# Four layers of attention in one hand-ordered kernel: a new order of its instructions, and another way through the last four rows of output

## The chip, the core and the metric

The kernel runs on one core of one Trainium2 chip. Its time is device microseconds (us) of one launch, the median of several runs. The engines of the core each have an instruction stream of their own and meet through semaphores: TensorE (PE, matmuls; PEld is its loading of weights), VectorE (DVE), ScalarE (ACT), GpSimd (POOL) and SyncE (SP), which issues the transfers.

## What is computed

Four times, with two sets of weights in turn, a layer norm, an attention with 32 query heads of 16 dimensions and one head of keys and values, and an output product added to the input. One layer, cut to what matters:

```python
q = (x @ wq).reshape(B, S, H, Dh).transpose(0, 2, 1, 3)      # S 2048, H 32, Dh 16
k = x @ wk
v = x @ wv
scores = jnp.einsum("bhqd,bkd->bhqk", q, k) * (Dh ** -0.5)
p = _softmax(scores, axis=-1)
o = jnp.einsum("bhqk,bkd->bhqd", p, v)
return o.transpose(0, 2, 1, 3).reshape(B, S, H * Dh) @ wo
# used as
x = x + _A_ref(_layernorm(x), A_wq, A_wk, A_wv, A_wo)        # then B, then A, then B
```

x is 2048 x 512 in float32.

## The kernel before

**Tiles.** A layer's 2048 queries are four blocks `b` of 512. A block's heads are four groups `m` of eight. One (layer, block, group) is a pair, and there are 64 of them. For a pair the keys go by in halves; one unit is 128 x 1024 scores: eight small matmuls (64 x 32 pieces of the array, 512 columns each) into one of two score tiles `st`, each of two PSUM banks. ScalarE turns a unit into exponentials in a tile `pt` of SBUF (line 765). TensorE then multiplies these with the values and adds into two banks, `acc[0]` for even heads and `acc[1]` for odd ones (function `pv`). The values' tile has ones beside it, so the same product yields the sum by which the softmax divides; in `acc` each 32 rows hold 16 of values and 16 of sums.

**Two engines for the exponential.** There are 4096 units. For most ScalarE does the work. For some VectorE does it instead: TensorE writes their scores into a bank of their own, `by_v`, in two halves; VectorE reads each half (`exp_first`, line 796) and then works six steps on the unit (`chain`, lines 807 to 815).

**Everything else.** The projections for the next block or layer, layer norm, transposes and output products run in between, in program order of a work list (`plan`). They share one bank, `beside`. A product can be cut in row halves of the array (24 steps, laid beside other small matmuls) or be 12 whole passes of 128 x 128 (`whole`, line 521). VectorE's part of the list evacuates `beside`. Each output row block of 128 rows is a product of 12 passes (four groups `m`, three passes each, since both factors are split in a float16 value and a rest), and `out_add` (line 455) adds it to `x` and sends it out (line 460 in the last layer, by SP's queue).

**The order.** All of this is written out by hand in a string `ORDER`, one letter for each step, and every engine executes its part in that order. The letters that matter here:

- S: a unit of scores and its exponential on ScalarE.
- a to e, l to q: products with the values (E and O in `STEPS` are `acc[0]` and `acc[1]`), with row halves of a list product (M, N) beside them. f to k, r and s also write a half of a unit for VectorE (V, W).
- I: VectorE reads such a half. 0 and 1: one of the six steps for a unit.
- X: the next step of VectorE's list. F: a small whole step of TensorE's list. P: one whole pass.
- G: an evacuation of `acc` into `sum` (lines 902 and 904). D: a step of a division. Q: a load of queries. Y: a touch of `beside` by VectorE, by which the order between the two row halves is known.

**Divisions.** When a pair is complete, its sums are inverted and spread over the rows by transfers (`divide`). For the last pair `divide_last` does it without transfers: with `lo` and `hi`, masks of the rows, VectorE parts values (`ev`) and sums (`den`), and for each of four slices of 128 columns inverts, swaps halves of 16 rows by a shuffle, multiplies, casts to float16 and subtracts for the rest (lines 968 to 972). Then the four last row blocks follow, each as 12 P and an X, all through `beside`. The end of the order before is

```python
"...SSaaSSaaSSaaaaGGDDDDDDDDDDDDDDDDDDDDDDDDPPPPPPPPPPPPXPPPPPPPPPPPPXPPPPPPPPPPPPXPPPPPPPPPPPPXX"
```

The functions that the diff touches and what calls them, with the line numbers of the profile:

Of the kernel before, what the change touches and what calls it, by code (L numbers as in the profile page):

```python
# [23 lines left out]
NL = 4  # L24
# [36 lines left out]
    "aIqS0as0SaaISc0qSaq1Sa0qSaa1SQqq0Saa0ScqSaXaXSGlSXFGrSXaISaXa0SaSaX0aSsaXISaX0SaaXXS0ppp0Sa0QaSb0SaaS0aS"
    "cGoGSqj0SccIScsYSbIpS0ap0Sa0aSb0SaaS0aSaa0SQpaXSaXaSaSabGSppGpSkbISbhSIpaY0Sc0qSa0aSc0Saa0ScqSa0aScSQcaX"
    "SaXSaaSbGpSbpSGkppISahSIap0Sa0aS0dSaY0aScq0SaaS0cSccSQqqqSaXaXSaSabGSbpSGkpISbfSIbp0SaY0aS0aSaa0ScqDS0aa"
    "Sq0qSccDSQcqSaXaXSaSaaSFGSXalXGSppDSaDaDSbpSbbSbSdaYScqSaaSaSQaaSaqSaXaXScGqSXcDXSmGmSqaSqjaISasSaISDa0a"
    "XS0lXSa0aSlrXSaIaXSsXSQaaSSIaaXXSrGSGlXSaDbS0bpSbD0pSbbDSlYDq0ScqSIaa0Si0ScIc0SjcSD1aaXSa0SaaXSa0pSb1bSD"
    "bp0SbSbIaYDSc0qSaDaSDc0Scc0ScqSaXaD0SmSsXaISbb0S0kbISb0bSaDSa0aSjcIScDj0SaaDSc0SaaISa0qSi0aISc0SaaY1Ska0"
    "SaaXSa0SaaXSa0SFISaXa0Sb0ShbISb0pSkb1Sa0aSa1Sc0cSQaISa0aScr0SaaIScGqSjGo0SaSa1a0SapSaIaXSaDXSa0gSIbp0Sha"
    "D1Sa0Saa1Sc0Scc1ScqSc0qSaYIaS0bSaa0SkbISa0hSaISbDaSXa0SaXaS0kbISb0hSa1Sa0aSc1qSa0aSc1qSc0SccSIaY0SkbpISb"
    "0SaaXSa0SaaXSa0jScIc0Si0SccISa0qSjaY1Sa0aSb1Sa0aSbIpSp0bSaa0SkbISQa0pSaaXSa0SaaXSfGSGFISaXaSXkpSaaSbIpSX"
    "bX0b0Sb0ShaY1Sc0qSaaXS0cSaXaSXc0SccISaXqS0as0SaaISaXS0aaSaXS0aaSXa0rSaSIaXaSXaSasSaaISXXS0aa0SP0PSa1aS0P"  # L70
    "PSP1PS0PPSr1PPSP0SPSIaXaS0aSbb0SkaISa0aSkaISa0Sh0aISa0kSaa1Sb0Saa1Sb0SaaY1Scq0ScqScIc0SQcSaXa0SjcSIcc0Sa"
    "r0SaISbGb0Sa0pSpppGSpg0SaaISa0Scc1Sa0qSaaY0Sb0SdaXSaXXSaDXaXSDraISaXXaSDaXXSa0aSaX0sSaaISaXD0Saa0Sa0SaXa"
    "XS0FSaXSaDaXSaXrSDFISXaaDSaXSXaaXD0SFSXsaISaXm0SFSaXS0aaSrXaISa0aSD0kbISb0Shb1Sb0SbaY1ScDqSa0aScDq0ScqSI"
    "cqDSaXaXSa0SaaSXQa0SaaXS0aSaXlGSFGsSXmISaX0aSfXDSIaaXX0Sc0qSc0cScD0SicISaY0kSbp1Sb0bSbISbDaSXraISaXaDSc0"
    "ScDc0SjcS1cq0SaaY1Sb0Saa1SbpSa0aSbISa0aSb0sSaaISb0SgaISa0pS0aaXSa0SaaXSa0qScj0SccISc0qSjaISaY0aS0kbISb0S"
    "hb1Sb0Saa1Sa0pSaa1SpaXSa0SaaISaXsSaIc0SjcS1Qc0SaaS1a0SbaSIbGpSkGpppISb0ShaY1Sa0Saa1ScDq0SaaS1cSaXaSD0aSa"
    "IaXSa0sSaaISF0SarXSaDpS0bbSbIp0Sa0Sa0aScs0SaaISc0Sic1Sc0qSaaISa0Sb0bSaY0rSaaISc0SaaXSa0kSbbISa0S0aa0SjcI"
    "Sc0qSia1Sa0Saa1Sb0SbbISa0pSaYa0SjcISc0SaaXSa0rSaaISb0Sb0b0SkppSIQaa0Skpp1SaY0ScaS1cqGSqGqqq0ScSeIaXSa0rS"
    "ccISc0Saa1Sj0cSaa1Sa0SbbISb0pSbb0SkaISa0SaaY1Sja0SaaISc0SaXaXXSaDsXXSaISaXXaSDaXXSaDaX0SaSaX1m0SaSaD1mXS"
    "aX0SFSXa0SaaXSaXSaDa0SaSDF0SaXSaDaSXaXSaX0aSF0SrISaXaSsXaISF0SaXS0aaXSa0jScIcS0aSaa0SkbISQa0aSbk0SbISa0l"  # L80
# [1132 lines left out]
```

## Time and profile before

| what | value |
|---|---|
| median of 3 runs | 3518.9 us (3518.32 to 3522.29) |
| the profiled execution's own time | 3517.96 us |
| its span | 3516.1 us |
| mean granted TensorE clock | 0.997 |
| TensorE busy | 96% |
| VectorE busy | 94% |
| ScalarE busy | 98% |

The span goes from the first to the last instruction that the profiler recorded; the execution's own time has 1.9 us more around it. A busy share says only that some instruction of the engine was under way. Neighbouring instructions of one engine overlap a little, so the time that one takes in a queue is the distance of two starts, which is less than its own duration. In a row of the timeline stand start, duration, engine, line, operation, written and read tiles, shape and count; in brackets the idle time before it and who ended it.

### The profile page before, as it was taken

Reading aid. Unit: us, or ns where it says so; the run is one execution under the profiler, and the core shown is the slowest. Engines: PE = TensorE matmul, PEld = TensorE weight load, DVE = VectorE, ACT = ScalarE, POOL = GpSimd, SP = SyncE. Lnnn points to the kernel's source line nnn. Section 1 sums busy time; section 2 is a strip of 40 time slices with the busy share of each in tenths; the row PEclk is TensorE's granted clock in tenths of the full one; section 3 lists DMA queues with packets and bytes.
Section 4 is the critical chain, followed back from the end, with each engine's and each line's share of the span. In section 5 each row is a group of like instructions: output and inputs, shape, how many; then the busy total and the mean of one; then the engine's idle time right before and its main releaser. Section 6 shows DMA issues by size and latency. Waiting matters only on the chain.

```text
span 3516.1 us, 202447 instructions
## 1 busy us (share of the span) xinstructions
PE 3386.4 (96%) x95867; PEld 2007.0 (57%) x95867; DVE 3314.7 (94%) x4511; ACT 3428.6 (98%) x3722; POOL 152.6 (4%) x110
## 2 busy tenths in 40 slices
PE   7999999999999999999999999999999999999997
PEld 3566566464566666646456666655546666454543
DVE  4979999999989999999998999999999899999994
ACT  6999999999999999999999999999999999999996
POOL 1001000000000100000000000000000010000000
PEclk9999999999999999999999999999999999999999
DMA  3121111110012111101001211110101211110100
GB/s 93 63 73 49 43 45 36 37 43 28 26 43 64 43 55 33 43 25 45 19 29 56 58 48 40 41 41 22 46 20 45 56 40 39 44 39 25 34 29 20
DMA packets 92738, 147.54 MB, mean 42 GB/s; under 512 B 30008, under 2 KB 46392, under 8 KB 91896
## 3 DMA queue, kind: packets, MB, share of 16 engines
q1 hardware_dynamic: 91896, 134.49, 12.7%
q8 instruction: 751, 12.30, 1.4%
q14 instruction: 91, 0.75, 0.1%
HBM read 90.57 MB, written 34.59 MB: 36 GB/s over the span
## 4 chain that ended last, share of the span: by engine, by line
PE 49%; ACT 38%; DVE 10%; issue 2%; DMA 1%; SPq 0%; POOL 0%; DVEq 0%; POOLq 0%
ACT pt L765 38%; PE acc L484 24%; PE st L484 13%; PE beside L484 9%; PE by_v L484 2%; DVE pt L796 1%; DVE pt L807 1%; DVE poly L815 1%; DVE poly L813 1%; DVE poly L814 1%; DVE mant L810 1%; PE beside L382 1%; DVE pt L812 1%; PE beside L521 1%; DVE wq L339 1%
## 5 line engine op out<-in xcount | busy, mean ns | idle before, releaser
L765 ACT ACTIVATE pt<-st 128x1024 f32<-128x1024 f32 x3716 | 3424.4, 1082 | 33.4 <-PE st L484 27.7
L484 PE MATMUL acc<-pt,vop 64*32 64x256 f32 (+1 forms) x49712 | 2795.9, 444 | 6.0 <-DVE sum L902 3.7
L484 PE MATMUL st<-qt,kop 64*32 64x512 f16 x29728 | 1699.6, 380 | 76.4 <-ACT pt L765 52.7
L484 PEld LDWEIGHTS <-kop 64*32 64x32 f16 x32768 | 797.0, 90 | 1034.3 <-issue 768.0
L484 PEld LDWEIGHTS acc<-pt,vop 64*32 64x32 f32 x49712 | 1213.2, 106 | 255.6 <-DVE sum L902 11.6
L796 DVE TENSOR_SCALAR pt<-by_v 128x512 int32<-128x512 f32 x760 | 519.3, 683 | 40.3 <-PE by_v L484 29.4
L815 DVE SCALAR_TENSOR_TENSOR poly<-poly,mant 128x1024 f32<-128x1024 f32 x380 | 464.6, 1223 | 0.9
L807 DVE SCALAR_TENSOR_TENSOR pt<-poly,pt 128x1024 f32<-128x1024 f32 x380 | 464.3, 1222 | 0.6
L814 DVE SCALAR_TENSOR_TENSOR poly<-poly,mant 128x1024 f32<-128x1024 f32 x380 | 462.6, 1217 | 1.4
L813 DVE SCALAR_TENSOR_TENSOR poly<-mant 128x1024 f32<-128x1024 f32 x380 | 462.5, 1217 | 0.0
L484 PE MATMUL beside<-xnT,wq 64*32 64x512 f16 x5856 | 430.9, 376 | 3.1 <-DVE gv L425 1.8
L484 PE MATMUL beside<-wo,ot 64*32 64x512 f16 x5664 | 416.5, 376 | 2.2 <-DVE xt L457 0.9
L484 PE MATMUL by_v<-qt,kop 64*32 64x512 f16 x3040 | 302.6, 377 | 6.2 <-DVE pt L796 4.1
L812 DVE TENSOR_SCALAR pt<-pt 128x1024 int32<-128x1024 int32 x380 | 260.9, 687 | 2.6
L810 DVE TENSOR_SCALAR mant<-pt 128x1024 int32<-128x1024 int32 x380 | 260.4, 685 | 1.9
L484 PEld LDWEIGHTS <-wq 64*32 64x32 f16 x5856 | 175.4, 92 | 61.3 <-issue 14.7
L484 PEld LDWEIGHTS <-ot 64*32 64x32 f16 x5664 | 169.1, 92 | 53.0 <-issue 8.2
L433 POOL TENSOR_TENSOR sq<-qs 128x512 bf16<-128x512 f16 x64 | 97.5, 1523 | 901.3 <-DVE qs L430 872.5
L902 DVE COPY sum<-acc 128x512 f32<-128x512 f32 x128 | 84.2, 683 | 44.2 <-PE acc L484 43.0
L484 PE MATMUL beside<-xnT,wkv 64*32 64x512 f16 x1344 | 97.6, 376 | 0.6 <-DVE xnT L390 0.5
L369 POOL TENSOR_TENSOR rstd<-var,nhalf 128x4 f32<-128x4 f32 x16 | 28.2, 1761 | 1336.2 <-DVE var L368 1336.2
L430 DVE TENSOR_SCALAR qs<-beside 128x512 f16<-128x512 f32 x63 | 43.1, 684 | 28.9 <-PE beside L484 15.6
(108 smaller groups left out, 819.9 us busy)
## 6 DMA issues: line engine op xcount, KB each, us to landing
qt<-qs SPq DMA_DIRECT2D x85, 512.0 KB
qs<-qs SPq DMA_DIRECT2D x128, 128.0 KB
rec<-rs SPq DMA_DIRECT2D x63, 256.0 KB
xs<-xt SPq DMA_DIRECT2D x48, 256.0 KB
xt<-xs SPq DMA_DIRECT2D x48, 256.0 KB
xt<-in_A_x_dram SPq DMA_DIRECT2D x32, 256.0 KB
sum<-sum SPq DMA_DIRECT2D x252, 32.0 KB
out_dram<-xt SPq DMA_DIRECT2D x16, 256.0 KB
```

Of the source, the lines that this page charges most:

```text
L430: V.tensor_scalar(qs[:, 0], ps, BIG, -BIG, ALU.min, ALU.max)
L433: G.tensor_tensor(sq, qs[:, 0], qs[:, 0], ALU.mult)
L484: PE.matmul(o[32 * j:32 * j + 32], w[j][h], x[j][h], start=start, stop=stop, skip_group_check=True, tile_position=(64 * r, 32 * j))
L765: e = A.activation(pts[:, i], st[s], AF.Exp, scale=SCALE / UP / UP).ins
L796: w = V.tensor_scalar(e[:, 512 * r:512 * r + 512], by_v, SCALE / UP / UP * LOG2E * 2.0 ** 23, LEAD, ALU.mult, ALU.add).ins
L807: writer[i] = V.scalar_tensor_tensor(p, poly, C0, p, ALU.add, ALU.mult).ins
L810: lambda: V.tensor_scalar(mant.bitcast(I32), e, 0x7FFFFF, 0x3F800000, ALU.bitwise_and, ALU.bitwise_or),
L812: lambda: V.tensor_scalar(e, e, 0x7F800000, None, ALU.bitwise_and),
L813: lambda: V.scalar_tensor_tensor(poly, mant, C3, mant, ALU.add, ALU.mult),
L814: lambda: V.scalar_tensor_tensor(poly, poly, C2, mant, ALU.add, ALU.mult),
L815: lambda: V.scalar_tensor_tensor(poly, poly, C1, mant, ALU.add, ALU.mult),
L902: V.tensor_copy(sums[pr, odd], acc[odd])
```

## The change

Three things are changed.

- The string `ORDER` is another one from its 43rd letter on. By letters: S 3716 to 3718, I 760 to 756, P 96 to 120, X 779 to 774, G 170 to 168, D 339 to 315, Y 132 to 127. Its end is now `"...SSaaSSaaSSaaaa"`.
- The last pair's evacuation and division, and the last four output row blocks, are no longer in the order and the work list. A function `finish` issues them after the order's end. It reads `acc` where it lies, ScalarE scales and casts, the four row blocks have a bank each (`beside`, `by_v` and the two of `st[0]`), and the passes of groups 0 to 2 of a row block are issued ahead of the passes of its last group.
- The last row block goes out in two halves of 64 rows, by SP's queue and ScalarE's.

The diff, without the string:

```diff
@@ out_add
-        if l == NL - 1:
+        if (l, t) == (NL - 1, NT - 1):
+            for h, eng in enumerate((SP, A)):
+                h = slice(64 * h, 64 * h + 64)
+                eng.dma_start(out[t * P:(t + 1) * P, :][h], x[h])
+        elif l == NL - 1:
             SP.dma_start(out[t * P:(t + 1) * P, :], x)
@@ plan
-                add_outputs(l, b, wo)
+                if (l, b) < (NL - 1, NB - 1):
+                    add_outputs(l, b, wo)
@@ add_sums
+        if pr == len(pairs) - 1:
+            return
...
-                (divide_last if pr == len(pairs) - 1 else divide)(pr)
+                divide(pr)
@@ divide_last goes, finish comes
+    def finish():
+
+        l, b = NL - 1, NB - 1
+        den = one.tile([P, BQ], F32, name="rec")
+        r = one.tile([P, BQ], F32, name="tmp")
+        ev = one.tile([P, BQ], F32, name="sum03")
+        banks = [beside, by_v, st[0][:, 0:512], st[0][:, 512:1024]]
+        begin_ot(l, b, NM - 1)
+        o = ot[l, b, NM - 1]
+        cs = [slice(P * t, P * t + P) for t in range(4)]
+
+        def products(t, ms):
+            for m in ms:
+                for n, (w, x) in enumerate(three([p[:, cs[t]] for p in ot[l, b, m]],
+                                                 [p[:, m] for p in wt["wo", l]])):
+                    PE.matmul(banks[t], w, x, start=m + n == 0, stop=m == NM - 1 and n == 2)
+
+        def invert(c):
+            V.reciprocal(den[:, c], den[:, c])
+
+        def times(c):
+            V.stream_shuffle(r[:, c], den[:, c], swap)
+            V.tensor_tensor(ev[:, c], ev[:, c], r[:, c], ALU.mult)
+            A.copy(o[0][:, c], ev[:, c])
+
+        def rest(c):
+            V.tensor_tensor(o[1][:, c], ev[:, c], o[0][:, c], ALU.subtract)
+
+        first, last = range(NM - 1), (NM - 1,)
+        products(0, first)
+        products(1, first)
+        A.activation(den, acc[0], AF.Copy, scale=hi)
+        V.scalar_tensor_tensor(den, acc[1], lo, den, ALU.mult, ALU.add)
+        A.activation(ev, acc[0], AF.Copy, scale=lo)
+        invert(cs[0])
+        V.scalar_tensor_tensor(ev, acc[1], hi, ev, ALU.mult, ALU.add)
+        times(cs[0])
+        invert(cs[1])
+        rest(cs[0])
+        products(0, last)
+        products(2, first)
+        times(cs[1])
+        invert(cs[2])
+        rest(cs[1])
+        products(1, last)
+        products(3, first)
+        out_add(l, 4 * b, banks[0])
+        times(cs[2])
+        invert(cs[3])
+        rest(cs[2])
+        products(2, last)
+        out_add(l, 4 * b + 1, banks[1])
+        times(cs[3])
+        out_add(l, 4 * b + 2, banks[2])
+        rest(cs[3])
+        products(3, last)
+        out_add(l, 4 * b + 3, banks[3])
@@ after the order's last letter
+        finish()
```

More of the change, by code (lines that the diff above doesn't have):

```diff
@@ L61 @@
[L61 to L80, printed above, removed]
@@ L191 @@
[L191 to L194 removed]
+    "XSSPPPPPSPPSPPPSPPSXaSXaaSbpSbbSbpSapSpaYSaqSaaSoQqSccqqcaXaaXalGSPGPSPPSPPPSaSPPPSaSaaSPQPSXaaXSaSaSaaS"
@@ new lines @@
+    "FSXaaXSXXSaXXaSXXSaXXaSGQSGlXSaXmSFSXaSXaaXSFSXaSXaaXSXFSXaSXaaSFSXQaSXaaSbpSalGSppGSbbSbpSaYSccScqSccSq"
+    "aXSaXSaXaXSXFSXaXXSQaXXXaSXaXSXaXaXSXmGSmXXlGSgISaaXSrXmISF0SaXa0SaXSaXm0SaSF0SaXaS0aSQaXaSXX0SFSXaaXSGS"
+    "rGFISaXSgXaISb0pSb0b0SbSb0dSaY0SacS0cqSQccScqSaXSXaaXSXFXSaXSXaXaXXXSrGSGlISaXXaSaXXSaXXaSXsXaISa0aS0aSX"
+    "QaXa0SFSXa0SaaSXaXSrGFISaXSsGlISaXaSXaX0Saa1SF0SaSXa0aSXaS0aQmS0FSaXSa0aSaXSGmqjGScISc0iScISa0a0Sqq0qSaa"
+    "Y0SbpSb0Sbb0SQbpSaXaXSaXSFXaXSaXXSaXXfXSIppGpSgaISbGSb0b0Sb0pSaaY0SaSa0aSc0qSQccScScaSqaXSaXaSrbISbSgGlI"
@@ new lines @@
+    "SbGpS0bb0Sa0Saa0ScqSa0aSc0SQccScqSaYaSpaXSaXSgaISbGrSbIb0SpGpSp0pb0SaSaY0aScq0SaaS0cSQccScqSaXaXSaSbaSak"
+    "SaIbGSrmISa0ScGc0Sc0qSaa0SaSb0bSbp0SQaaYSaSccSqaXSaXaSraISmGsSIFSXaaX0ScGSc0a0SaqSa0aSa0Saa0SQapSaXaXSbX"
+    "DpXSaSabGShISbppGSgDpISaXaY0ScXSa0a0SaqSXa0qSaaXScXSQaaSaqXDSaXaSDmGSmXaDSjcGScIqDqS0aSaa0SkbISb0bS0kbIS"
+    "b0SaaYD0SaqSQc0cSaXSa0aSaXSaDjqGSqqGScIcDSj0cISaDaSDi0SaIaY0SrbSa1a0SbSa1aD0SbpS1aaS0bSaaIS0apSbDaSXaDSa"
+    "XaDSiDqISc0qjSa1Sa0aSbISb0b0SkppSIbp0SaaSD1a0SicS1cq0SaaISaXSaDaSXaDS0arSaIaDSF0SaaXSf0Scc1Sc0qSccISm0q0"
@@ new lines @@
+    "SaSaY0aSbs0SbbISb0ShbISa0pSaXa0SaXSa0aSQcq0SicISc0qSjc1Sa0SamYGSbIpSpGn0pSb0Saa0SbpSaXaDSXa0SakSaIa0SkbS"
+    "IbbD0S0hpISb0SaaY1Sa0qSaa1Sc0Scc1ScqS0qeSaXa0SaSaXaDSa0jSaaISc0SicISc0qSi0cISa0SaaY0ShpSbIb0SkbS1b0SaaSI"
+    "paXSa0aXSa0SfaISa0Saa1SF0SaaXSaXjScSccXX0ScqSaIc0Sa0SaaYXSa0pSQaaXSapXSa0pSapXSabGSb0SappGSgISaXaS0kaISa"
+    "XSaaXS0apXSaSaXaSaSaXmXSm0SPPP0SPPr0SPPSIPP0SPPS0PaXSa0Sb0aSa0kSaaISa0ShaISa0pSak0SaIa0Sb0ShbISa0pSaaY1S"
+    "c0Saa1Sc0qScj0SaaISc0ScaXSa0sSaaISb0ShbISb0pS0aa0SkbSId0SaaYS1aq0Scc1Sc0Scc0SaqSaXaXXSQaDSXXaaDSaXXrSDaI"
@@ new lines @@
+    "aXXSa0SalGSsGSmIaXD0SaSaX1aS0arSaIaXSaXS0F0SaaXSaDSaXaXSsDaISFDSXaaDXSaXSaX0aSF1SXarD0SaaXSa0SFSIaaXS0aS"
+    "Xaa0SkbISb0pkSa1Sa0aSc1Sa0aScIqSaDa0ScScDc0SaqDSaYr0SbbISd0SaaXSaXSa0aXSa0rSXaIlXSF0SaaX0SaSgXISaX0aSrmX"
+    "XS0apSbIb0Sa0SQa0aSc0sSaaIScGqSGjq0SaaS1c0qScSaIaYDS0kbISb0bSaXSaD0aSrlXSa0qSc1cS0aSaIaS0bpDSb0kSbbISbD0"
+    "SaaSYDaj0Saa1Sc0SccISaXSa0aXSa0SgaISb0pSkb1Sb0bSb1SaY0aScISc0cScr0ScaISc0SaaXSa0rSaaISaXSa0b0Sb0pSbb0Skb"
+    "SIa0SaaSY1aj0SccISc0Sc0cSaq0SaaXSa0SQaaXSa0sSaaISFGSXmr0ScISa0cGSc0sSaaISa0Shb1Sb0pSbDb0SbSaIaY0Sa0qSicI"
@@ new lines @@
+    "ScD0SaaXSa0rScc1Sc0qScISaDa0Sa0sSbbISb0Sbh1Sb0pSaaY1Sc0SaaISa0qSaaXS0aSicISc0jSc1cS0cSaYIaS0bs0SaaISb0Sa"
+    "aS1kb0Saa1Sb0SaaISb0pSaaXSa0ShbISa0kSa1aS0aSccIS0cr0SccSIQc0SamSY1rb0Saa1SbGSb0bSlGSlIaXSaXXSaDaXXSaDSaX"
+    "XaDSXXaS0aaSXa0sSaImSXD0aSa1mS0fSaIlXSaXSa0aDSa0SgaISmD0SfaDSF0SlXS0SISaXaSXa0SF0SXaa0SaSXaaXSX0FSaXsSaI"
+    "aXSa0SF1SaXa0SaSaXaS0a0jSccISc0SicISc0SaaY1Sb0pSbb0Sh0SaaISb0sSaIaS0bSaaXSXQar0SaaSIaXSa0aXSFGsGSlISaXa0"
+    "SaXSDaX0aSmX0SaaSXaXD0Sar1Sa0aSISa0a0SsSaIaDSr0SaaDS0aSaDS0aaSIS0aa0Sa0SsaISa0aSr1Sa0aS1Sa0aSIS0agSmIS0a"
@@ new lines @@
+    "aS1ar0SaSa1a0SSIaa0SsSIaa0Sar1Sa0Saa1S0SaaIS0sSaIaS0rSaa1S0aSa1Sa0aSISa0gSmIS0QaaSr1S0aaSGSGl0SaaISa0SaD"
+    "s0SamISa0SaaD1Sa0rSaa1S0SaaIS0sSaIaSDaS0fSaD0aSlDSa0aSqqIqSa0a0Sqq0SicISc0qSja1SaYa0Sbp1Sb0pSbbISb0SaaXS"
+    "a0SicISa0jSa1aS0cqSaISa0a0SkaSIbb0Skb1Sb0SbaYS1aq0ScaISc0SaaXSa0rSccISa0Sfa1Sc0qSaaIS0cq0SQcSaY0aSkbISa0"
+    "aSbGpSkGl0SaSaIa0SbDp0Sb0aSaXSa0aSjcDISc0cSjc1Sc0SaaYISb0k0SaSaIaDSkb0Saa1Sa0pSa1Sa0aSbIpSa0aSb0SaaXSaXX"
+    "rSaIaXXSaDSXaXaDSrXXSa0aSX1SaX0aSISa0aXSaXs0SaSFI0SaaXSf0SalXSXS0FSISaXa0SaXSaXaX0Sa0sSFISaXa0SaSaXa0SaS"
@@ new lines @@
+    "1QF0SaaXSa0SaXa0SajSqGqqGScIcS0cSiaISDa0jSaaY1Sb0SbbISaD0pS0kaSaIa0SbSh1a0SaSaDa0SaSaIaDS0spISaXaSXlDSFX"
+    "a0SaSfX0aSlXSa0SaaX0SaSaIaX0SsXSIaXaX0Sa0Sar1Sa0aS1Sa0aS1Saa0SSIa0SasSaIa0Sar1Sa0SaaIS0Sa0gSaISa0rSa1aS0"
+    "mSa1aS0SaIa0SQsSaIa0SfSa1lGSGSm0aSa1Sa0SaIaSDl0sSaIaS0rSaD1aS0aSa1Sa0aSIS0asSaIaDSa0rSaaDS0SaDaS0SaIaS0s"
+    "SIaa0S0aSa1rSa0aS1Sa0aS1Saa0SSIa0aSgISa0mSa1Sf0SaaIS0l0SgSaIa0SaSa1a0SmS1aa0SrSIaa0SsSIaa0Sa1Sf0Saa1S0lS"
+    "aISa0SQgaISm0rSa1aS0SGSGl0SaaISa0SaDa0SsaISa0SaaD1Sm0Saa1Sa0Sar0SaaIS0SaaDSa0SasDSaIaDSr0qSaaISc0qS0cq0S"
@@ new lines @@
+    "icISqq0SfaY1Sa0pSbb1Sb0SbbISa0pSaaXSa0SicISc0jSc1cS0cSaYaIS0bp0SbpSQb0bSb0SaaXSa0sSbbISlGpS0kaISa0pShGbI"
+    "Sa0Saa1Sa0jSaa1Sc0Saa1Scq0SaaSIc0SciSIaq0Saa1Sa0SaaYS0a0kSaaISd0SaaXSa0jScISc0cSfqISa0a0Sa0qSiqISa0qSaa1"
+    "Sa0SaaY1Skb0SaaISb0Sbb0SbpSQaXaXXSl0SaaXXSlGSrGmISaXXaS0aSaXaXS0lSX0aaX0SrSIaa0SasXSaISXF0SaaXSa0SraISaX"
+    "aSXa0SF0sXSaISaXaXSaX0SF1SaXa0SaSaXa0SFSXaS0aSaXa0SP0PSaa0SPPS0PPSa0aSaSPPPSPPPSXaSXaaXSXFXSQaXaXSXaXXSa"
+    "bSaSaaSgGpISbGShbISb0pS0aa0SpaYS0aSa0aScq0SaaScSQccScqSaXaXSaSbGpSGkppISbhSIbp0Sa0aS0aSaY0aScq0SaaSDc0Sc"
@@ new lines @@
+    "cSQcqSaXaDXSaSapSGbbSpGppSpbSahSIaYSgcISc0qSDjcIScDc0SaXSDaaXSQs0aSbIbSDb0Shb1Sb0pSaaY1ScGqS0cSmGmSIqc0S"
+    "iaISa0SiaD1Sa0qSaa1Sa0SaaISa0SaaDSa0qSaXaSDaXSaDaDSa0rSFISaXaX0ShSaIa0Sb0pS0aaSa0SccD0SaSaX0aSkbISaXaXSk"
+    "0bSIbXSaYDaS0cqDSa0aScXqDSaXqS0arSaIaXSq0SaaXSrXSaaSXSXaa0SISaXaS0ap0Sb0pSaa0SkppISb0pShp1SQaY0SacSIcq0S"
+    "a0aScGqSsGqqISqa0SjaXSaDaXSa0Scc1Sc0qSccISaD0q0SaSaY0aSkbISa0aSkb1Sb0pSbIpSaXa0SaXSa0aSbDpS0hbSbISDb0aSk"
+    "aDSa0aSaISc0c0Sc0qSjcISc0aSa1SaYa0SkaXSa0aSaISaXaS0raISF0SaXaS0aShb1S0bpSb1bS0bSaYIaS0csSaIa0ScSi1c0ScqS"
@@ new lines @@
+    "a1a0ScSaIaXSQa0SaaXSa0jSaqISmGqjGSc0Scc1Sa0qSaaISa0Sb0bSb0sSbbISbD0SaaSY1aj0SaaISaXSaD0aSXas0SccISc0Sic1"
+    "SaDSa0aSb1pS0aaSaISc0aSa0qSaaY0ShSbIb0SkbSIpaXSa0lXSa0Sc0jSccISa0jSa1aS0aSb1bS0bSbIbS0bSaY0aSc0ScaSXas0S"
+    "aaISaXSa0a0SF0SgaISaXSaX0jSQcIcS0ajSa1a0SaSbGppGSppIpSaXa0SbXSaaXSb0pSaaYXSaq0SasSaIqXSa0rSaaXScqXSa0Sal"
+    "ISaXqSaXSa0aS0bp0SkbpISb0Sga1Sl0Scqq1Sqq0qSqqqIqSa0Saa0SjaSIaaY0SkbS1aXSa0aSapISa0a0ShSaIa0SbkSa1a0SaSa1"
+    "a0ScqSIcc0SjcISc0SaaYS1a0kSbb1Sa0SaaISb0SaaXSa0rSbbISQb0kSa1Sa0aScGqScIq0Sa0aSfGSbIbS0dSaY1aS0jcSa1a0ScS"
@@ new lines @@
+    "eIaXSaXXSaDaXXSaDSaXXlDSXXas0SaSaIaXD0SlSaX1a0SrlS1aaXSX0SFSIaXSaDaSXaXSaDa0SaSDFD0sSaSIaaXSr0SXSXXD0SFS"
+    "IaXSa0aSXa0Sa0aSsaISF0SaXaS0aSaaXS0ajScIcSDa0SaDa0SbDsSaIa0SkbS1b0SbbS1a0pSQaaY1ScSa0aScISa0aScGqSGrmISa"
+    "XaSXa0SaaSXFDXS0aaSaXS0alXD0SaX0SaaSX0aSaXaX0SknISb0SalDSrbISbDk0SbIaYSDa0Sc0cScr0SccSIc0SaaSXa0SamXSa0r"
+    "SbIb0Sb0pSkbISb0SaaY1Sjc0Saa1Sc0SccISc0qSaaXS0aSaaXSa0sSbIbS0bkSbISb0a0Sa0pSarY0SaaSIc0Sic1Sc0qSccISaXSQ"
+    "a0aXSa0rSbbISb0kSa1Sa0aSqqGqSoGc0ScSaIa0Sa0rSaaISaD0ShaS1ap0SaaD1Sb0SaaISa0SicISa0SaaY1SkaDSXaa0SaSaXa0S"
@@ new lines @@
+    "FSIaaXS0raISb0Shb1Sb0pSbb1Sa0SaaY1ScqS0cqScIc0ScSaXa0SscSaIa0SjcSIc0Sc0gSIcq0SaaYS1a0SbbS1bp0Sbb1ShSaXa0"
+    "ScqSIcq0SicISa0SQaaS1a0pSaa0Sa0SabGSb0kSaaISa0SrcGSeIlY0SaSb0bS0ak0SaaISd0SaaXSa0rSaaISc0SicISc0qS0ar0Sa"
+    "aISb0Sbb1Sb0pSpb1SaYa0SjcISa0qSaaXSaXXSaDXaXSsDaISaXaXSDaXXSa0aSaX1SaXD0aSm1Sa0aSmXSrXaISF0SaXaSDaSXaaXS"
+    "Da0SFDSaXa0SaSaXaXSsX0mSFISaXa0SaXSa0aS0FSQrXaISaXaS0aSimISGqoGSc0cSja1Sa0SaaISbD0pSa0aSb0pSkbISbD0pSaa1"
+    "Sa0SgaYISc0qSaXaXSaDSrXaISaXaDSXFDSaX0aSrXS0aaSaX0SaXSX0aaSIS0aa0Sg0SaImS0aSf1Sa0aS1lS0aaSIS0agSaIS0amS1"
@@ new lines @@
+    "ar0SaSa1a0SSIaa0SsSIaa0Sar1Sa0Saa1S0SaaIS0sSaIaS0rSaa1S0QaSa1Sa0aSGSGlISa0SgaISmD0Saa1Sa0SamD1Sa0Sar0Saa"
+    "IS0SgaISa0SarDSa0aSmISaDa0SsDSaIc0Sq0jqScc1Sa0Sam1Sb0pSb1bSb0SbdSIaY0SaiSIaq0SiaXSa0SccISa0Sa0a0SjcSIcq0"
+    "ScaS1a0SaaSY1ak0SaaISb0ShbISb0pShb1SaXSa0cSc1qS0ccScIq0SaSaY0aSQkbISa0aSh1Sa0aSbISa0lGSkGpSbIb0SarSXaaD0"
+    "SaqSa1q0SaSa1aD0SbSaIa0SkbSIbb0Sbp1SaYDSa0aSc1Sa0aSc0jSaaISc0SiaISa0jSa1Sa0aSaISa0aS0aqSaXlXXSsaDISaXXSa"
+    "DaSXXrl0SaaXSXl0SaaXS1XS0aaSI0SaXaXSF0SaXSa0aSaXSaXa0SFSXa0SgmISaXSaXaX0SF0SXaS0aaSXQraISF0SasXSaIaXSrGS"
@@ L195 @@
+    "SaIaS0rSa1a0SaSa1S0aaSIS0agSIm0Saa1SrGSGl0SaSa1a0SaSaImDS0asSaISa0aSaD1r0SaSa1a0SSaIa0SsSaIaDSa0SaDS0aaS"
+    "DS0aaS0S0aa0SS0aaSa0Sa0SaaSSaaSSaaSSaaSaSaSaaSSaaSSaaSSaaSSaaSSaaSSaaSSaaSSaaSSaaSSaaaa"
 )
@@ L906, in evac @@
                 return
-            if pr < len(pairs) - 1:
-                if pr not in dens_of:
-                    dens_of[pr] = dens.tile([P, 32], F32, name="den")
-                t = sums[pr, odd][16 * (1 - odd):P:32]
-                SP.dma_start(dens_of[pr][64 * odd:64 * odd + 64],
-                             t.rearrange("j (p q) -> j p q", p=16))
+            if pr not in dens_of:
+                dens_of[pr] = dens.tile([P, 32], F32, name="den")
+            t = sums[pr, odd][16 * (1 - odd):P:32]
+            SP.dma_start(dens_of[pr][64 * odd:64 * odd + 64], t.rearrange("j (p q) -> j p q", p=16))
             done.add(("s", pr, odd))
             if ("s", pr, 1 - odd) in done:
-                (divide_last if pr == len(pairs) - 1 else divide)(pr)
+                divide(pr)
         evacs.append(evac)
@@ L952, in divide @@
         divs.extend([invert, spread, lambda: V.tensor_tensor(ev, ev, r[0], ALU.mult), parts, rest])
-    def divide_last(pr):
-        l, b, m = pairs[pr]
-        ev, od = [sums.pop((pr, k)) for k in range(2)]
+    def finish():
+        l, b = NL - 1, NB - 1
         den = one.tile([P, BQ], F32, name="rec")
         r = one.tile([P, BQ], F32, name="tmp")
-        begin_ot(l, b, m)
-        o = ot[l, b, m]
-        divs.append(lambda: V.tensor_scalar(den, ev, hi, None, ALU.mult))
-        divs.append(lambda: V.scalar_tensor_tensor(den, od, lo, den, ALU.mult, ALU.add))
-        divs.append(lambda: V.tensor_scalar(ev, ev, lo, None, ALU.mult))
-        divs.append(lambda: V.scalar_tensor_tensor(ev, od, hi, ev, ALU.mult, ALU.add))
-        for c in range(0, BQ, P):
-            c = slice(c, c + P)
-            divs.extend([
-                lambda c=c: V.reciprocal(den[:, c], den[:, c]),
-                lambda c=c: V.stream_shuffle(r[:, c], den[:, c], swap),
-                lambda c=c: V.tensor_tensor(ev[:, c], ev[:, c], r[:, c], ALU.mult),
-                lambda c=c: V.tensor_copy(o[0][:, c], ev[:, c]),
-                lambda c=c: V.tensor_tensor(o[1][:, c], ev[:, c], o[0][:, c], ALU.subtract)])
```

189 lines of the change are left out of this document (70 added, 119 removed).

## Prediction

> **What bounds the kernel now.** I read the page first, then ScalarE's instructions in order of time, then what TensorE waited for, then the timeline of the end.
>
> ```profile
> span 3516.1 us, 202447 instructions
> PE 3386.4 (96%) x95867; PEld 2007.0 (57%) x95867; DVE 3314.7 (94%) x4511; ACT 3428.6 (98%) x3722; POOL 152.6 (4%) x110
> L765 ACT ACTIVATE pt<-st 128x1024 f32<-128x1024 f32 x3716 | 3424.4, 1082 | 33.4 <-PE st L484 27.7
> L796 DVE TENSOR_SCALAR pt<-by_v 128x512 int32<-128x512 f32 x760 | 519.3, 683 | 40.3 <-PE by_v L484 29.4
> L807 DVE SCALAR_TENSOR_TENSOR pt<-poly,pt 128x1024 f32<-128x1024 f32 x380 | 464.3, 1222 | 0.6
> L812 DVE TENSOR_SCALAR pt<-pt 128x1024 int32<-128x1024 int32 x380 | 260.9, 687 | 2.6
> ```
>
> Three engines are over 94% busy, but one sets the pace: ScalarE, whose 3716 exponentials (letter S of the order) fill 3424.4 us. VectorE computes 380 more (760 letters I, one for each half). ScalarE's own timeline shows where it was not fed:
>
> ```profile
> 0.75 1.28 ACT L388 ACT_TABLE_LOAD   x1 [0.75 <-PEq L1199]
> 25.98 0.59 ACT L1008 ACTIVATE vf<-kps 32x512 f32<-32x512 f32 x1 [7.79 <-PE kps L1006]
> 34.34 1.94 ACT L765 ACTIVATE pt<-st 128x1024 f32<-128x1024 f32 x2 [7.77 <-PE st L484]
> 37.53 13.23 ACT L765 ACTIVATE pt<-st 128x1024 f32<-128x1024 f32 x14 [1.24 <-PE st L484]
> 53.94 99.62 ACT L765 ACTIVATE pt<-st 128x1024 f32<-128x1024 f32 x108 [3.19 <-PE st L484]
> 825.05 213.39 ACT L765 ACTIVATE pt<-st 128x1024 f32<-128x1024 f32 x232 [1.05 <-PE st L484]
> 1243.84 8.78 ACT L765 ACTIVATE pt<-st 128x1024 f32<-128x1024 f32 x9 [1.19 <-PE st L484]
> 2961.92 522.37 ACT L765 ACTIVATE pt<-st 128x1024 f32<-128x1024 f32 x569 [0.94 <-PE st L484]
> ```
>
> So the run has three parts. The **start**, until 34.34 us. The **middle**, from there to 2961.92 + 522.37 = 3484.29. The **end**, 31.8 us after it. In its longest unbroken run ScalarE makes 569 in 522.37 us, 0.918 us each. At that rate 3716 need 3411.3 us; the middle takes 3450.0. It loses 38.7 us, of which 4.4 are the two gaps at the very start (1.24 and 3.19). What made TensorE late with the scores:
>
> ```profile
>   DVE sum L902: 15.3, 30
>   DVE pt L807: 8.3, 15
>   DVE pt L796: 4.1, 10
>   DVE gv L425: 1.8, 2
>   DVE sum L904: 1.6, 7
> ```
>
> These lines are from the view of L484, the helper behind all its tiled matmuls and weight loads: us and times that their engine sat idle until VectorE released it. They sum to 31.1 us. TensorE works in program order, so a wait for VectorE holds back the S behind it; two score banks forgive only part of it. Of the 34.3 us lost after the start I put two thirds, about 22, on VectorE coming late; the rest is stretches with too much TensorE work. The split is an estimate; its ends are 0 and 31.
>
> **The end, as it is.**
>
> ```profile
> 3482.73 2.71 PE L484 MATMUL acc<-pt,vop 64*32 64x512 f32 x32
> 3485.37 2.12 PE L521 MATMUL beside<-wo,ot 128*128 128x512 f16 x9
> 3485.46 1.29 DVE L902 COPY sum<-acc 128x512 f32<-128x512 f32 x2 [28.47 <-PE acc L484]
> 3487.18 0.75 DVE L962 SCALAR_TENSOR_TENSOR rec<-sum,half,rec 128x512 f32<-128x512 f32 x1
> 3487.85 0.48 DVE L963 TENSOR_SCALAR sum<-sum,half 128x512 f32<-128x512 f32 x1
> 3489.03 0.94 DVE L968 RECIPROCAL rec<-rec 128x128 f32<-128x128 f32 x1
> 3490.02 0.29 DVE L969 STREAM_SHUFFLE tmp<-rec 128x128 f32<-128x128 f32 x1
> 3490.35 0.29 DVE L970 TENSOR_TENSOR sum<-sum,tmp 128x128 f32<-128x128 f32 x1
> 3490.67 0.23 DVE L971 CAST ot<-sum 128x128 f16<-128x128 f32 x1
> 3490.93 0.29 DVE L972 TENSOR_TENSOR ot<-sum,ot 128x128 f16<-128x128 f32 x1
> 3490.96 0.82 PE L521 MATMUL beside<-wo,ot 128*128 128x512 f16 x3 [3.47 <-DVE ot L971]
> 3491.14 0.94 DVE L968 RECIPROCAL rec<-rec 128x128 f32<-128x128 f32 x1
> 3497.47 0.68 DVE L457 SCALAR_TENSOR_TENSOR xt<-beside,xt 128x512 f32<-128x512 f32 x1
> 3498.21 4.73 PE L521 MATMUL beside<-wo,ot 128*128 128x512 f16 x12 [6.43 <-DVE xt L457]
> 3503.73 2.75 PE L521 MATMUL beside<-wo,ot 128*128 128x512 f16 x12 [0.78 <-DVE xt L457]
> 3510.05 0.69 DVE L457 SCALAR_TENSOR_TENSOR xt<-beside,xt 128x512 f32<-128x512 f32 x1 [2.84 <-PE beside L521]
> 3510.77 0.33 SPq L460 DMA_DIRECT2D out_dram<-xt  x1
> ```
>
> T0, the end of the last product into `acc`, is 3482.73 + 2.71 = 3485.44. VectorE then works alone until 3497.47, all four slices before the first addition; after that matmuls and additions take turns on the one bank. The last addition ends at 3510.74, T0 + 25.3; 5.4 us of output and closing follow.
>
> **The new end, step by step** (us after T0). Spacings come from those starts. A 512-column combination: 3487.18 to 3487.85, 0.67. A reciprocal: 0.95. Shuffle 0.33, multiplication 0.32, subtraction 0.21 (3490.93 to 3491.14). An addition: 0.69. A pass of TensorE: 12 in 2.75 with a last one of about 0.38, 0.217.
>
> ScalarE scales `acc[0]` straight from its bank. No such row exists at this place; `vf` took 0.59 for as many columns, and I take 0.61. The two copies and both scalings are gone from VectorE: it combines from 0.65 to 1.32, inverts slice 0 until 2.27, combines `ev` until 2.94 (ScalarE's second scaling ended near 1.25), shuffles and multiplies until 3.59. Each cast moves to ScalarE: 128 columns, between VectorE's 0.23 and the 0.59 for 512; VectorE meanwhile inverts the next slice (0.95), so either end is hidden. Slice 1's reciprocal ends at 4.54, slice 0's subtraction ends at 4.83.
>
> TensorE meanwhile runs 9 + 9 passes for two rows, from -0.07 to 3.84; then the last three of row 0, whose third waits for the subtraction: 4.87. Nine of row 2 follow until 7.04, three of row 1 until 7.69, nine of row 3 until 9.64, three of row 2, the last ending at 10.45.
>
> VectorE: subtraction 4.75, slice 1 ready 5.40, reciprocal 6.35, subtraction 6.56, row 0 added 7.25, slice 2 ready 7.90, reciprocal 8.85, subtraction 9.06, row 1 added 9.75, slice 3 ready 10.40. Row 2 waits for TensorE, 10.47, and is added by 11.15. Slice 3's subtraction ends at 11.44, the last pass at 11.86, and row 3 is added by 12.57. That is 25.3 - 12.6 = 12.7 us earlier. `rest(cs[3])` and the last three passes stand behind the third addition, 0.69 us; without that place the end would come some 0.7 us sooner.
>
> The output of the last row is two halves, on SP's queue and on ScalarE's; nothing waits behind either. One issue takes 0.33 us in the row; the other queue has no row, so -0.3 to +0.5, and I take 0. The Trainium skill (DMA: Bandwidth & Descriptors, Issuing engines are not separate DMA queues) says that both queues run on the same 16 DMA engines and save issue time alone, which speaks against a gain here; no run shows it yet.
>
> Bounds of the end: -13.2 (no wait for TensorE, half an issue), and -7.7, if TensorE is at half speed (below).
>
> **The new order.** Counted over the letters: S 3716 to 3718, I 760 to 756, so two exponentials move to ScalarE: 2 x 0.918 = +1.8. The 48 P of the end go, but 72 more stand earlier: six products in whole passes instead of row halves, for the same TensorE time (12 x 0.217). The first 42 letters are the same, and the two gaps at the start stay nearly whole.
>
> The other letters are rearranged everywhere, so I count what decides VectorE's lateness, the room between its work and TensorE's next use. Between an I and the next scores into `by_v` there was no S in 5 places and one in 262; now 0 and 208. Between a product's last X and the next use of `beside`: 6 without an S and 92 with one; now 0 and 72. A G directly before the next `acc` product: 37, now 31. Together 402 narrow places become 311, 23% fewer. The second count is VectorE's load in each 20 stretches from S to S, every letter at its row less the 0.08 us by which neighbours overlap (two copies in 1.29 us): over 20 x 0.918 us in 23% of them, now 20%; over by 5% in 1.4%, now 0.6%. TensorE's load by the same count is unchanged.
>
> So fewer waits, not none: between 23% (the places) and 55% (the heavy stretches) of 22 us, 5 to 12; I take 7. Ends: 20 if nearly all go; a loss of 4, since a new order has places of its own that I cannot see.
>
> **Sum** against the profiled execution's 3517.96 (span 3516.1 and 1.9 around it): 3517.96 + 1.8 - 7 - 12.7 = 3500.1. The median of the runs is 0.94 above that execution, so 3501.
>
> **Rivals.**
> - The order brings nothing: VectorE is as full, and its waits only move. For it: the load falls by 3 points in a hundred only. 3518.9 + 1.8 - 12.7 = 3508. Chance 0.17.
> - The order recovers nearly all waits, 20 us: 3488. Against it: 208 narrow places for `by_v` stay. Chance 0.08.
> - TensorE falls to half speed at the end. In the rows, 12 passes took 4.73 us after a wait of 6.43, but 3 took 0.82 after one of 3.47; my longest wait is 0.9 us. It costs 2 us for each 12 passes, 5 us for the 30 after the first wait: 3506. Chance 0.06. The Trainium skill (TensorE: Matmul & The Clock Gate, Part 1) puts the drop after an idle window of about 3.4 us, which the 3.47 us row does not show; by either, 0.9 is too short.
> - Slower: the group ends. After a G TensorE must have `acc` free, and 31 places have no S between. If each of the 63 pair boundaries before the last costs 0.45 us more than now (a wait averages 15.3/30 = 0.51 there), that is 28 us, more than the end saves: 3518.9 + 1.8 - 12.7 + 28 = 3536. It outweighs the end from 0.17 us for each. Against it: those places became fewer. Chance 0.04.
> - A part of this, or another queue, eats most of the end's gain: 3512 to 3525. Chance 0.05.
>
> **How the numbers follow.** My forecast has 0.60. A measurement of this kernel can tell about 0.2%, 7 us, from no change. Faster takes the forecast and the first three rivals, 0.91, less 0.03 for their edges: 0.88. The same 0.08, slower 0.04. The range 3492 to 3510 takes in the forecast and the first and third rival, and leaves out the others and edges of these, 0.2.
>
> **What would show it.** ScalarE's last exponential should end near 3479, and 19.1 us should follow it instead of 31.8 in a span of near 3498; the last addition should end 12.6 us after the last `acc` product; the end's passes should keep 0.217 us, with no second table load on ScalarE (one row of 1.28 us now, Copy and Exp both after it). L484's waits for VectorE should fall below 31.1 by a quarter to a half. I am wrong if ScalarE's gaps stay at 34 us or grow, or if the end takes over 22 us.

## The result, and the profile after

The changed kernel takes 3497.07 us, the median of six runs (3493.64 to 3498.76), against 3520.43 for six runs of the old one (3518.32 to 3522.83): 0.9932 of it, 95% interval 0.9919 to 0.9945. The forecast was 3501, in 3492 to 3510. The profiled execution took 3498.76, the longest of the six, against 3517.96; the traces differ by 19.2 us, the medians by 23.4.

From the changed kernel's page, the span and the exponentials:

```profile
span 3496.9 us, 201941 instructions
L769 ACT ACTIVATE pt<-st 128x1024 f32<-128x1024 f32 x3718 | 3421.5, 1081 | 29.4 <-PE st L487 25.9
```

ScalarE in order of time:

```profile
34.31 1.94 ACT L769 ACTIVATE pt<-st 128x1024 f32<-128x1024 f32 x2 [7.99 <-PE st L487]
...
53.70 34.12 ACT L769 ACTIVATE pt<-st 128x1024 f32<-128x1024 f32 x37 [2.56 <-PE st L487]
...
2916.59 560.65 ACT L769 ACTIVATE pt<-st 128x1024 f32<-128x1024 f32 x610 [0.65 <-PE st L487]
3478.41 0.69 ACT L989 ACTIVATE rec<-acc,half 128x512 f32<-128x512 f32 x1 [1.17 <-PE acc L487]
```

The last exponential ends at 2916.59 + 560.65 = 3477.24 instead of 3484.29, though two more had to be made. By the measure of the prediction (0.918 us each) the middle loses 3442.9 - 3413.1 = 29.8 us instead of 38.7. The end is 3496.9 - 3477.24 = 19.7 us instead of 31.8. Together: 8.9 less loss, 1.8 more exponentials, 12.1 less end.

The end in order of time, cut to the rows that set it:

```profile
3475.67 2.71 PE L487 MATMUL acc<-pt,vop 64*32 64x512 f32 x32
...
3478.31 2.12 PE L973 MATMUL beside<-wo,ot 128*128 128x512 f16 x9
...
3479.13 0.75 DVE L990 SCALAR_TENSOR_TENSOR rec<-acc,half,rec 128x512 f32<-128x512 f32 x1 [29.26 <-ACT rec L989]
...
3480.27 2.11 PE L973 MATMUL by_v<-wo,ot 128*128 128x512 f16 x9
...
3482.37 1.07 PE L973 MATMUL beside<-wo,ot 128*128 128x512 f16 x3
3482.76 0.23 DVE L984 TENSOR_TENSOR ot<-sum,ot 128x128 f16<-128x128 f32 x1
...
3483.27 2.10 PE L973 MATMUL st<-wo,ot 128*128 128x512 f16 x9
...
3485.86 2.75 PE L973 MATMUL st<-wo,ot 128*128 128x512 f16 x12
...
3488.65 0.69 DVE L456 SCALAR_TENSOR_TENSOR xt<-st,xt 128x512 f32<-128x512 f32 x1 [0.83 <-PE st L973]
3489.26 0.28 DVE L984 TENSOR_TENSOR ot<-sum,ot 128x128 f16<-128x128 f32 x1
3489.40 0.81 PE L973 MATMUL st<-wo,ot 128*128 128x512 f16 x3 [0.78 <-DVE xt L456]
...
3490.24 0.69 DVE L456 SCALAR_TENSOR_TENSOR xt<-st,xt 128x512 f32<-128x512 f32 x1 [0.70 <-PE st L973]
3490.96 0.54 SPq L461 DMA_DIRECT2D out_dram<-xt  x1
3490.96 0.58 ACTq L461 DMA_DIRECT2D out_dram<-xt  x1
```

T0 is 3475.67 + 2.71 = 3478.38. TensorE waits 0.78 us at most and keeps its full pace (12 passes in 2.75 us); no 12 passes take 4.73 us as in the old kernel. The last addition ends at 3490.93, T0 + 12.55. After it come 6.0 us instead of 5.4. One row is not as I drew it: the last three passes write the second half of `st[0]`, yet all three waited for the third addition, which reads the first half. I call this a wait by tile; the variant with two tiles below tests it.

### The profile page after: what moved, and what is told of

The parts are those of the page before. It is cut to its first block, busy times and chain, and to the rows that moved or that the text cites. A ratio compares the mean times of both kernels' runs of the same rounds, so it can differ in the third digit from the quotient of the medians.

```text
span 3496.9 us, 201941 instructions
## 1 busy us (share of the span) xinstructions
PE 3383.4 (97%) x95611; PEld 2006.8 (57%) x95611; DVE 3297.6 (94%) x4482; ACT 3428.2 (98%) x3730; POOL 154.3 (4%) x110
## 4 chain that ended last, share of the span: by engine, by line
PE 53%; ACT 31%; DVE 12%; issue 3%; DMA 1%; SPq 0%; POOL 0%; DVEq 0%
ACT pt L769 31%; PE acc L487 27%; PE st L487 14%; PE beside L487 9%; PE by_v L487 2%; DVE pt L800 2%; DVE poly L817 1%; DVE pt L811 1%; DVE poly L819 1%; DVE poly L818 1%; DVE mant L814 1%; DMA qt<-qs 1%; DVE pt L816 1%; PE beside L524 1%; PE beside L381 0%
## 5 line engine op out<-in xcount | busy, mean ns | idle before, releaser
L487 PE MATMUL beside<-xnT,wq 64*32 64x512 f16 x5664 | 410.6, 376 | 0.8 <-DVE gv L424 0.8
L487 PE MATMUL beside<-wo,ot 64*32 64x512 f16 x5568 | 409.4, 376 | 0.0
L487 PEld LDWEIGHTS <-wq 64*32 64x32 f16 x5664 | 166.1, 92 | 46.4 <-issue 4.9
L908 DVE COPY sum<-acc 128x512 f32<-128x512 f32 x126 | 82.9, 686 | 14.8 <-PE acc L487 13.5
L487 PE MATMUL beside<-xnT,wkv 64*32 64x512 f16 x1056 | 76.0, 376 | 0.0
```

What stands on the lines that cost most here:

```text
L487: PE.matmul(o[32 * j:32 * j + 32], w[j][h], x[j][h], start=start, stop=stop, skip_group_check=True, tile_position=(64 * r, 32 * j))
L908: V.tensor_copy(sums[pr, odd], acc[odd])
```

## The experiments

Each states a loss: the time from the first exponential's start to the last one's end, less 0.918 us for each. The old order's is 38.7 us, the changed one's 29.8. The numbers in brackets behind a time are its ratio to the old kernel on the same chip and the 95% interval of that ratio.

**The end alone** (the changed functions, the old order without its last 79 letters):

```diff
-    "...aaGGDDDDDDDDDDDDDDDDDDDDDDDDPPPPPPPPPPPPXPPPPPPPPPPPPXPPPPPPPPPPPPXPPPPPPPPPPPPXX"
+    "...aa"
```

> The new end behind the old order (3716 exponentials on ScalarE). My account: the end is worth what the traces show of it, 31.8 us after the last exponential less 19.7, about 12.2 us, and it does not depend on the order: 0.9965 of before, 3508. The middle, from the first to the last exponential, stays at 3450 us. Rival, the order does it all through a better arrival at the end: under 6 us. Rival, the end does it all and the order nothing: 0.9933, 3497.

3510.3 us against 3521.35 on the same chip (0.9970, 0.9959 to 0.9981): 11 us. In its trace the end is 19.3 us (12.55 to the last addition), the loss 42.8. So the end brings what the trace shows of it; the middle of the same order differs by 4 us between these two traces.

**The order alone** (the old functions, the changed order with those 79 letters behind it):

> The new order with the old end (G, D, P and X as before, one bank). My account: the middle takes 3443 us instead of 3450 though it has two exponentials more, so 7 us less by the profiles, up to 11 by the medians: 3509 to 3513. With the end alone it should add up to the whole change. Rival, the order brings nothing: 3520 to 3522. Rival, the parts need each other: their sum misses the whole by over 5 us.

3510.34 us (0.9969, 0.9956 to 0.9981): 11 us as well. Its loss is 29.5 us, as in the changed kernel. The two parts add to 22 us, the whole is 23: they do not need each other. The kernels below that keep the new order and change only the end have losses of 25.8 to 27.9 us, so the 29.8 of the changed kernel's trace is the largest of seven single traces, and 8.9 us is the least that they give for the order.

**A lighter VectorE**, in both kernels:

```diff
-            lambda: V.scalar_tensor_tensor(poly, poly, C1, mant, ALU.add, ALU.mult),
+            lambda: None,
```

> The old kernel with one of VectorE's six steps for a unit left out (the third of the polynomial's four, 1.13 of about 6.95 us), so that VectorE's units take a sixth less; the exponentials of these units are other numbers. If VectorE's lateness is two thirds of ScalarE's 38.7 us of loss, the loss falls to 12 to 18 us and the time to about 3497. If TensorE's own load or the transfers set it, the loss stays above 30 us.

> The changed kernel with the same step left out. If the new order gains through VectorE, the two orders become alike: a loss of 12 to 18 us here too, and the difference of the two light kernels is the end's 12.2 less the 1.8 of two exponentials, about 10.4 us. If the new order gains by something else, the difference stays at 19 to 23 us.

3503.84 us (0.9950, 0.9934 to 0.9965) and 3490.30 us (0.9914, 0.9899 to 0.9929). The exponentials' rows, first the old order's, then the new one's:

```profile
L765 ACT ACTIVATE pt<-st 128x1024 f32<-128x1024 f32 x3716 | 3419.5, 1087 | 23.6 <-PE st L484 19.6
```

```profile
L769 ACT ACTIVATE pt<-st 128x1024 f32<-128x1024 f32 x3718 | 3417.3, 1085 | 22.6 <-PE st L487 19.7
```

The losses are 23.9 and 18.8 us. Some 15 us of the old order's loss went with a sixth of VectorE's work on its units, so VectorE is a main cause; but I expected 12 to 18 to be left in both, and more stayed. The orders came nearer, from 8.9 us of loss apart to 5, and in time to 13.5 us apart, between the 10.4 of my account and the 19 of the rival.

**Thinner list products**, in both kernels (`both`, for the bank `beside`):

```diff
-                    PE.matmul(o[32 * j:32 * j + 32], w[j][h], x[j][h], ...
+                    k = slice(256 * (turn[0] % 2), 256 * (turn[0] % 2) + 256) if bank == "beside" else slice(None)
+                    PE.matmul(o[32 * j:32 * j + 32, k], w[j][h], x[j][h, k], ...
```

> The old kernel with every row-half matmul of a list product on 256 of its 512 columns, halves in turn, so that the projections and output products are other numbers. It takes some 170 us of work off TensorE (12864 such matmuls, eight side by side in 0.213 us, half of it) and leaves the letters, VectorE and all waits in place. With VectorE a sixth lighter 24 us of ScalarE's 38.7 us of loss were left. If what was left is TensorE's load between two S, the loss falls here by 10 to 20 us. If it is neither, it stays above 36.

> The changed kernel with the same thinner products. If the new order's gain is VectorE's lateness alone, it gains here as much over the old order as before, 9 to 13 us of loss. If part of it is a better spread of TensorE's load, the two come nearer: 3 to 8 us.

3516.42 us (0.9988, 0.9978 to 0.9997) and 3494.87 us (0.9925, 0.9909 to 0.9940); the losses are 36.6 and 26.1. TensorE's busy time in the old kernel, from which 170 us should have gone, fell from 3386.4 by 24, and its wait for ScalarE rose from 52.7 to 57.7:

```profile
PE 3362.8 (96%) x95867; PEld 1934.4 (55%) x95867; DVE 3313.5 (94%) x4511; ACT 3425.0 (97%) x3722; POOL 151.4 (4%) x110
...
PE st L485 <- ACT pt L766: 57.7, 172, 0.5
```

In the old kernel's trace 12127 of these 12864 matmuls run at the same time as a product with the values on the other row half, which lasts as long without them. So this edit gave TensorE little room, and it does not tell whether its load matters, although the loss stayed above the 36 us that I had set as the mark for "neither". The orders stay 10.5 us of loss apart.

**Thinner products with the values**, in the old kernel:

```diff
+                    if bank[0] == "acc":
+                        size = x[j].shape[1] // 2
+                        k = slice(size * (turn[0] % 2), size * (turn[0] % 2) + size)
```

> The old kernel with each product of exponentials and values on half of its columns, halves in turn, so that sums and outputs are other numbers. The thinner list products mostly lay beside such products on the other row half and freed little; these stand on TensorE's own path, half of some 1750 us. Letters, VectorE and all semaphores stay. If VectorE's lateness alone makes ScalarE's loss, 30 us or more of the 38.7 remain. If lateness costs only because TensorE has no room left to catch up, or if TensorE's load makes a part itself, the loss falls below 20 us although VectorE is as late.

A single run: 3503.25 us, beside one of 3524.66 for the old kernel on that chip, and a loss of 24.5. Now TensorE had room: its busy time fell to 3034.8 us. VectorE was as busy (3312.9 us, 3314.7 before) and as late: TensorE's waits for it in the middle, matmuls and weight loads together, sum to 51.5 us (51.7 before):

```profile
PE st L488 <- ACT pt L769: 270.7, 840, 0.5
...
PE by_v L488 <- DVE pt L800: 10.0, 23, 1.1
```

```profile
L769 ACT ACTIVATE pt<-st 128x1024 f32<-128x1024 f32 x3716 | 3413.1, 1201 | 30.7 <-PE st L488 27.4
```

Here the busy time and the idle time of the row move apart. ScalarE is idle for 30.7 us, against 33.4 in the old kernel: the long waits for VectorE still reach it. But the busy time fell from 3424.4 to 3413.1, near the 3411.3 of an undisturbed run: what went are small delays of each exponential that overlap with the one before and so are counted as busy. So the loss has two parts, gaps and small delays. With room for TensorE some 11 us of 13 of the small delays went, and few of the gaps. The light kernel shows the other side: gaps fell by 9.8 us, small delays by 4.9. So the gaps follow VectorE's lateness more than TensorE's load, while the small delays follow both. The loss came out between my two cases (30 and 20), so neither stands alone. The changed kernel was not run with this edit.

**Variants of the end**, one run each of the changed kernel with one edit:

```diff
# one queue
-        if (l, t) == (NL - 1, NT - 1):
...
-        elif l == NL - 1:
+        if l == NL - 1:
# VectorE alone
-        A.activation(den, acc[0], AF.Copy, scale=hi)
+        V.tensor_scalar(den, acc[0], hi, None, ALU.mult)
...
-            A.copy(o[0][:, c], ev[:, c])
+            V.tensor_copy(o[0][:, c], ev[:, c])
# no lead
-        products(0, first)
-        products(1, first)
...
-        products(1, last)
-        products(3, first)
+        products(1, range(NM))
# two tiles
-        banks = [beside, by_v, st[0][:, 0:512], st[0][:, 512:1024]]
+        banks = [beside, by_v, st[0][:, 0:512], st[1][:, 0:512]]
```

> The changed kernel with its last row block sent whole by SP's queue, as before. The span after the last addition was 5.35 us in the old kernel and 5.95 in the changed one, where an issue took 0.54 and 0.58 us instead of 0.33. If the split is what costs it, this comes back to 5.3 to 5.4. If it is the rest of the end (four rows close behind each other), it stays at 5.9. The time from the last acc product to the last addition stays at 12.55.

> The changed kernel with VectorE doing the two scalings and the four casts of the end itself. My account: VectorE is the longer chain of the end, so it takes 0.6 us more for the second scaling and 4 x 0.26 for the casts, less some wait for TensorE at the third addition: 13.8 to 14.2 us from the last acc product to the last addition instead of 12.55. Rival, TensorE's passes set the end: 12.5 to 12.8.

> The changed kernel with each row's twelve passes in one piece, the four banks and ScalarE's share kept. TensorE then sits idle from about 2 to 4 us after the last acc product and runs 36 passes after the first row's, 7.8 us: the last addition ends at 13.7 to 14.0 us instead of 12.55. Rival, VectorE's chain alone sets the end: 12.5 still.

> The changed kernel with the fourth row's bank taken from the other score tile. In the changed kernel the last three passes began only when the third addition had ended, though they write another bank. If the wait is by tile, two of them now run ahead, the third starts right after slice 3's subtraction, and the last addition ends 0.2 to 0.3 us sooner, 12.3 us after the last acc product. If it was something else, nothing moves.

| kernel | T0 to the last addition, us | after it, us |
|---|---|---|
| old | 25.3 | 5.35 |
| changed | 12.55 | 5.95 |
| one queue | 12.55 | 5.49 |
| VectorE alone | 13.56 | 5.95 |
| no lead | 14.49 | 6.12 |
| two tiles | 12.33 | 6.02 |

ScalarE's share is worth 1.0 us, less than I expected of it (13.8 to 14.2 without it); the lead of the passes 1.9, more (13.7 to 14.0). What else the end gained has no run of its own. From the run without the lead, T0 being 3474.13 + 2.71, the piece after the third addition:

```profile
3474.13 2.71 PE L487 MATMUL acc<-pt,vop 64*32 64x512 f32 x32
...
3487.85 2.75 PE L973 MATMUL st<-wo,ot 128*128 128x512 f16 x12 [0.78 <-DVE xt L456]
3490.64 0.69 DVE L456 SCALAR_TENSOR_TENSOR xt<-st,xt 128x512 f32<-128x512 f32 x1 [2.64 <-PE st L973]
```

Here the wait by tile costs more: twelve passes stand behind an addition whose bank they do not touch. With two tiles the same place becomes

```profile
3485.11 0.28 DVE L984 TENSOR_TENSOR ot<-sum,ot 128x128 f16<-128x128 f32 x1
3485.45 0.39 PE L973 MATMUL st<-wo,ot 128*128 128x512 f16 x1 [0.55 <-DVE ot L984]
```

Two passes ran ahead and the third waits for its operand alone: the wait was by tile, and it cost 0.2 us.

**A better end**: two tiles, one queue, and

```diff
-        out_add(l, 4 * b + 2, banks[2])
-        rest(cs[3])
+        rest(cs[3])
+        out_add(l, 4 * b + 2, banks[2])
```

> The changed kernel with three edits at its end: the fourth row's bank from the other score tile, slice 3's subtraction ahead of the third addition, and the last row whole by SP's queue. VectorE no longer waits with the subtraction for TensorE, so the third pass of the last row follows the third row's passes directly: the last addition ends 11.5 to 11.7 us after the last acc product instead of 12.55, and 5.4 us follow instead of 5.95. 1.4 us less than the changed kernel by the trace, which its spread of 5 us between runs will hide: 0.9925 to 0.9935 of before, if its middle is the same.

The last 15 passes run in one piece and the last two additions follow each other:

```profile
3483.63 3.40 PE L969 MATMUL st<-wo,ot 128*128 128x512 f16 x15
...
3486.42 1.34 DVE L456 SCALAR_TENSOR_TENSOR xt<-st,xt 128x512 f32<-128x512 f32 x2 [0.17 <-PE st L969]
```

The last addition ends 11.6 us after T0, 0.9 sooner, as expected; 5.7 us follow, where I expected 5.4. 3495.27 us (0.9929, 0.9915 to 0.9942): by its time not to be told from the changed kernel's 0.9932, as expected.

## Why the prediction was right

**The end.** Forecast 12.7 us sooner to the last addition, measured 25.3 - 12.55. The sum of the steps held to 0.02 us, but by errors that cancel, which is luck. ScalarE's scaling took 0.69 instead of 0.61; yet VectorE's next steps follow each other more closely than I spaced them, and slice 0's subtraction ended at T0 + 4.61 instead of 4.83. TensorE, which waits for it, was done with row 2 at 10.23 instead of 10.45, and the addition started at 10.27 instead of 10.47. Then the wait by tile, which I had not seen, gave 0.2 back. No half speed came, and no second table load.

**The output in two halves.** I took 0 between -0.3 and +0.5. The seven profiles with a split last row have 5.6 to 6.1 us after the last addition, 5.93 on average; the seven that sent it whole have 5.3 to 5.7, 5.39 on average. Five of the latter have the old end; the two with the new one have 5.49 and 5.67, so the split costs some 0.3 to 0.5 us. The Trainium skill (DMA: Bandwidth & Descriptors, Issuing engines are not separate DMA queues) says that two issuing engines save issue time alone. The traces agree that nothing more is gained, but of the issue time they show the reverse, 0.54 and 0.58 us for the halves against 0.33 for the whole.

**The order.** Forecast 7 us of loss less, measured 8.9 by the two profiles, and 11.0 by the time of the order alone, where 5.2 net had been forecast: the term was too small, and the median fell 4 us below the forecast for it. By the two parts of the loss, the gaps after the start fell from 25.6 to 21.4 us and the small delays from 13.1 to 8.4: both parts shrank, though TensorE's load was not made lighter. The direction and VectorE's part in it hold: with VectorE lighter the orders' distance shrinks to 5. That the rest of this distance is VectorE's as well is not shown.

**One step failed.** I expected TensorE's waits for VectorE in the view of the matmul helper to fall from 31.1 us by a quarter to a half. The same lines are now

```profile
  DVE sum L908: 16.0, 40
  DVE pt L811: 7.6, 15
  DVE pt L800: 2.4, 7
  DVE sum L910: 1.9, 6
  DVE kop L404: 1.0, 2
  DVE gv L424: 0.8, 2
```

28.7 us without the line of `kop`, the keys, which is new: 8% less. The narrow places became fewer, but the sum of waiting hardly fell. What fell are the long waits. Counted over matmuls and weight loads in the middle that waited over 0.15 us for VectorE, the sum is 51.7 us in the old kernel and 52.2 in the changed one; those over 0.6 us were 21 with 19.6 us and are 12 with 9.6. The two runs of the parts repeat it: 21 with 19.7 in the old order, 11 with 8.9 in the new one.

ScalarE's starts show that these made the difference. Call an exponential late by the distance of its start from the one before, less 0.918 us; this sums to 38.4 us in the old kernel and to 29.6 in the changed one. The exponentials that start within 1.5 us after the end of a wait of over 0.6 us hold 13.6 us of it in the old kernel and 5.6 in the changed one, so 8.0 of the 8.8 us that went. The runs of the parts have 13.6 (old order) and 5.1 (new one).

If a matmul's wait and its weight load's at the same time are taken as one, the old kernel has 19 long waits and 86 shorter ones. Within 1.5 us after 16 of the 19 an exponential starts behind a gap of over 0.15 us, but after only 8 of the 86. So most short waits do not reach ScalarE; that the second score bank takes them up is my explanation, and no run tests it. Of the 19, 5 stood before `beside`, 2 before `by_v`, 6 before `acc` behind an evacuation and 6 before `acc` for VectorE's exponentials. The changed kernel has none, none, 7 and 3, and 1 for the keys. So the long waits that went stood at `beside` and `by_v`, where no place without an S was left, and in part before VectorE's exponentials, which I had not counted; those at the group ends, counted from 37 down to 31, did not become fewer. The step that took the number of narrow places, and the sum of waits that should fall with it, as the measure was wrong in kind, and it was partly luck that its 7 us came near.

**The lateness share.** Of 34.3 us after the start I put 22 on VectorE. The lighter VectorE took 15 away and the lighter TensorE 14, and both were still in play afterwards, so the loss is made by the two together; a clean split is not shown. Unforeseen as well: TensorE now waits 3.1 us in five places for queries to land before it writes `by_v`, where the old profile had 0.7 in one and the run of the end alone, with the old order, 2.4 in two. Whether these loads come too late for VectorE's units was not tried.
